# Gated linear attention and a silu feed-forward layer: the fast path's instruction order made with another machine model

## The chip, the cores and the metric

The kernel runs on one core of a Trainium2 chip. The metric is device time in microseconds (us) of one execution, taken as the median of several; a profile is taken of one more execution. The engines are named PE (TensorE, matmuls; PEld are its weight loads), DVE (VectorE), ACT (ScalarE), POOL (GpSimd) and SP (SyncE, which here issues nearly all loads).

## The reference

A gated linear recurrence runs over 768 time steps for 4 batches and 8 heads of width 48; its output, laid out as 3072 tokens of width 384, goes through a feed-forward layer with silu of width 2048.

```python
for t in range(S):
    state = alpha[:, :, t, :, None] * state + np.einsum('bhd,bhe->bhde', k[:, :, t], v[:, :, t])
    y[:, :, t] = np.einsum('bhd,bhde->bhe', q[:, :, t], state)
...
h = x @ w_in
g = h * (1.0 / (1.0 + np.exp(-h)))
return (g @ w_out).astype(np.float32)
```

Everything reaches the chip in wide form: the weights are 64-bit floats that the kernel rounds to 32 bits itself.

## The kernel before

There are two paths. `quotients` is the fast one, valid when the decay factors keep within bounds; it computes a flag `within` while it runs. `general` follows in a conditional that is entered only when the flag says so, which these inputs do not cause. All that the profile shows is `quotients`.

The work is cut into 24 chunks of 128 time steps of one batch (six chunks a batch, the batches taken in turn), and four chunks make a token group; there are six groups. A step of the program's loop handles one chunk in stages:

- `products` transposes alpha, k and q so that time lies along the free axis, scans alpha into running products `u` (L734) and multiplies them into k, which gives `kp` (L745 for early chunks, L749 and L751 later); `quotient` takes reciprocals (L762), scans the inverse, `p` (L764), and multiplies q into it (L770). For the first eight chunks PE transposes (L392). From the ninth on DVE does it (L708, tiles `al` and `turn`), and there is one buffer for `al`, one for `u` and one for `turn`.
- `flip` (from the ninth chunk) writes a transposed `kp` (L780) to DRAM (L782, `flips`), and `land` (L790) reads it back as `kn`.
- `scores` forms the 128 x 128 score blocks on PE; ACT copies them (L812, L818, L821) and POOL masks them (L813, L825). `values` forms the outputs, which ACT copies to `xt` (L863); `states` adds to the recurrent state (L880, DVE).

Between the stages, `fill` issues pieces of the feed-forward layer in proportion to the work that is due. Groups 0 and 1 use plain products with w_in (`enter_plain`, silu L923). Groups 2 to 5 use a scheme with 20 block products in place of 24 (`enter`): it needs sums of blocks of w_in (`sums_w`, tiles `wx` and `w_in`) and of x (`sums_x`, tile `xc`, lines L582 to L587, all on DVE), and combines the products with ACT copies (L950) and DVE additions (L958) before the silu (L955). `PRODUCTS` gives the block of w_in and the block of x of each product. The fourth product, the first of the second piece of `enter`, reads block 15 of x; on PE it follows the first piece and one product of `leave`. Block 15 is the sixth sum of the second part of `sums_x`:

```python
SUMS_X = (
    (9, 1, 2, 1, 4), (6, 1, 0, 1, 2), (7, 1, 2, 1, 3), (8, 1, 0, 1, 7), (10, -1, 1, -1, 8),
    (11, 1, 5, -1, 10), (12, 1, 4, 1, 11), (15, -1, 0, 1, 12), (16, 1, 1, -1, 15),
    ...
PRODUCTS = (
    (11, 9), (3, 6), (14, 6), (18, 15), (5, 11), (17, 8), (9, 14), (7, 10), (10, 3), (19, 12),
```

`leave` multiplies with w_out in seven products per half group, in two PSUM banks (`ps_o`, 192 columns); ACT copies two of them (L1073, L1078), DVE forms u2 (L1088, L1090), u3 (L1099) and the outputs (L1056), and subtracts blocks of g (L1047, L1033 before it). A product that adds into a bank, or starts a new sum in it, waits until the reader of that bank is done.

`audit` reads alpha and the weights once more and reduces their extremes on DVE (L697).

What sets the order: the language's scheduler makes one list per engine, from program order as priority and a simulated run in which a machine model says when an instruction could start. Some instructions are kept in program order by hand: once the early buffers are released (`settle`, after the eighth chunk), all PE instructions are, so PE's order from there is the written one. Sums, audits and a few more are kept likewise; the rest of DVE's, ACT's, POOL's and SP's order is the scheduler's. PE's calls are all recorded at L388 (matmul) and L392 (transpose).

## Time and profile before

| | |
|---|---|
| median of 3 executions | 556.64 us (555.98 to 558.58) |
| the profiled execution | 557.26 us, of which its span is 555.5 us |
| granted PE clock, mean | 0.999 |
| PE busy | 541.4 us (97%), 5026 matmul records |
| weight loads busy | 489.7 us (88%) |
| DVE busy | 445.4 us (80%), 801 instructions |
| ACT, POOL busy | 208.5 us (38%), 76.1 us (14%) |
| DMA | 70.09 MB, mean 126 GB/s |

The span runs from the first instruction to the last; the execution's own time is 1.8 us longer. A group or a row of the timeline gives the start, the busy time, engine, line, operation, the tile written and those read, shapes and the count; in brackets stands the engine's idle time before it and what ended it. One fp32 matmul instruction leaves two records.

### The profile page before, as it was taken

What the parts mean: (1) busy time and instruction counts of PE and PEld (TensorE: products, weight loads), DVE (VectorE), ACT (ScalarE), POOL (GpSimd) and SP (SyncE); (2) the same over time, 40 slices, a digit from 0 to 9 for tenths busy, and PEclk for the clock granted to TensorE, in tenths of its full rate; (3) what the DMA queues carried; (4) which work ended last, traced back from release to release, by engine and by line L of the source; (5) the groups of instructions that cost most, each with busy time, mean ns of one, the idle gap of its engine ahead of it and who ended that gap; (6) DMA issues with size and microseconds to landing.
All of it is one profiled execution on the core that took longest, in us unless ns stands there. A gap on an engine that the chain in (4) does not pass through costs nothing. (4 is left out here: it accounts for less than half of the span.)

```text
span 555.5 us, 12640 instructions
## 1 busy us (share of the span) xinstructions
PE 541.4 (97%) x5026; PEld 489.7 (88%) x5026; DVE 445.4 (80%) x801; ACT 208.5 (38%) x466; POOL 76.1 (14%) x146
## 2 busy tenths in 40 slices
PE   6999999999999999999999999999999999999996
PEld 4788887998899999899999999988998999999996
DVE  5897788974999899997998986998884796945431
ACT  2556653223333253353353353344263342332100
POOL 3210000222210212021011021021121000001000
PEclk9999999999999999999999999999999999999999
DMA  9998971164454625355545654617642135500000
GB/s 215 246 249 210 232 195 33 47 161 116 117 136 125 159 63 138 86 145 149 139 112 139 193 139 120 191 27 183 170 137 91 54 91 169 172 11 22 10 24 30
DMA packets 99217, 70.09 MB, mean 126 GB/s; under 512 B 56272, under 2 KB 88656, under 8 KB 99152
## 3 DMA queue, kind: packets, MB, share of 16 engines
q1 hardware_dynamic: 97232, 65.30, 45.1%
q0 software_dynamic: 1920, 3.93, 2.0%
q8 instruction: 40, 0.66, 0.5%
q14 instruction: 25, 0.20, 0.1%
HBM read 61.34 MB, written 7.86 MB: 125 GB/s over the span
## 5 line engine op out<-in xcount | busy, mean ns | idle before, releaser
L388 PE MATMUL ps_o<-w_out,g 128*128 128x192 f32 x768 | 134.0, 328 | 0.5 <-DVE o L1056 0.5
L388 PEld LDWEIGHTS ps_o<-w_out,g 128*128 128x128 f32 x768 | 125.6, 190 | 3.5 <-DVE o L1056 1.0
L388 PE MATMUL ps_m<-xt,w_in 128*128 128x256 f32 x480 | 113.6, 383 | 1.5 <-ACT xt L863 1.1
L388 PEld LDWEIGHTS ps_m<-xt,w_in 128*128 128x128 f32 x480 | 89.1, 190 | 14.4 <-ACT xt L863 1.6
L388 PE MATMUL ps_o<-wt,g 128*128 128x192 f32 x576 | 99.7, 326 | 0.0
L388 PEld LDWEIGHTS ps_o<-wt,g 128*128 128x128 f32 x576 | 95.1, 190 | 1.6 <-issue 0.2
L388 PE MATMUL ps_m<-xc,w_in 128*128 128x256 f32 x288 | 70.7, 382 | 0.0
L388 PEld LDWEIGHTS ps_m<-xc,w_in 128*128 128x128 f32 x288 | 53.7, 190 | 7.0 <-DVE g L958 0.3
L1047 DVE TENSOR_TENSOR g<-g 128x512 f32<-128x512 f32 x72 | 50.1, 709 | 8.3 <-PE ps_o L388 8.3
L955 ACT ACTIVATE g<-g 128x1024 f32<-128x1024 f32 x32 | 33.1, 1056 | 61.2 <-DVE g L958 61.1
L1059 POOL DMA_DIRECT2D out_dram<-o x40 | 22.0, 551 | 219.5 <-DVE o L1056 113.7
L825 POOL TENSOR_SCALAR_AFFINE_SELECT g<-g 64x256 f32<-64x256 f32 x64 | 34.9, 546 | 124.4 <-ACT g L818 105.7
L388 PE MATMUL ps_m<-xc,wx 128*128 128x256 f32 x192 | 50.1, 383 | 1.0 <-DVE xc L586 1.0
L950 ACT COPY g<-ps_m 128x512 f32<-128x512 f32 x64 | 36.6, 588 | 37.0 <-PE ps_m L388 36.9
L388 PEld LDWEIGHTS ps_m<-xc,wx 128*128 128x128 f32 x192 | 35.2, 190 | 5.2 <-ACT u L1078 1.2
L958 DVE TENSOR_TENSOR g<-ps_m,g 128x512 f32<-128x512 f32 x56 | 37.1, 683 | 3.2 <-PE ps_m L388 2.7
L734 DVE TENSOR_TENSOR_SCAN u<-al,one 128x516 f32<-128x516 f32 x24 | 29.8, 1240 | 11.9 <-ACT al L731 11.6
L923 ACT ACTIVATE g<-ps_m 128x512 f32<-128x512 f32 x32 | 19.1, 597 | 41.7 <-PE ps_m L388 41.4
L950 ACT COPY part<-ps_m 128x512 f32<-128x512 f32 x32 | 18.9, 590 | 38.0 <-PE ps_m L388 24.0
L697 DVE TENSOR_REDUCE seen<-bits 128x1 f32<-128x512 int32 (+1 forms) x33 | 26.3, 823 | 5.7 <-DMA bits<-in_moe_w_in_dram 5.7
L764 DVE TENSOR_TENSOR_SCAN p<-al,inv 128x516 f32<-128x516 f32 x24 | 29.9, 1247 | 1.0 <-PE ps_a L388 0.3
L1056 DVE TENSOR_TENSOR o<-ps_o,u 128x192 f32<-128x192 f32 x24 | 8.5, 355 | 25.7 <-PE ps_o L388 22.8
(129 smaller groups left out, 648.5 us busy)
## 6 DMA issues: line engine op xcount, KB each, us to landing
bits<-in_moe_w_in_dram SPq DMA_DIRECT2D x24, 512.0 KB, 4.7
bits<-in_moe_w_out_dram SPq DMA_DIRECT2D x16, 384.0 KB, 3.9
at<-in_alpha_dram SPq DMA_DIRECT2D x64, 96.0 KB, 2.5
kt<-in_k_dram SPq DMA_DIRECT2D x64, 96.0 KB, 2.6
qt<-in_q_dram SPq DMA_DIRECT2D x64, 96.0 KB, 2.7
bits<-in_alpha_dram SPq DMA_DIRECT2D x9, 512.0 KB, 4.0
out_dram<-o POOLq DMA_DIRECT2D x40, 96.0 KB, 2.4
flips<-turn SPq DMA_DIRECT2D x12, 256.0 KB, 2.4
```

The lines of the kernel that those rows point to most:

```text
L388: in_order(nc.tensor.matmul(*args, **kw))
L697: dve.tensor_reduce(seen[kind][which][:, i : i + 1], x, axis=AX, op=op, apply_absolute_value=True))
L734: dve.tensor_tensor_scan(u[:, end - 1 :: -1], sg[:, end:0:-1], one[:, end:0:-1], 0.0, ALU.mult, ALU.add)
L764: dve.tensor_tensor_scan(p[:, 0:end], sg[:, 0:end], iv[:, 0:end], 0.0, ALU.mult, ALU.add)
L825: gps.affine_select(x, x, pattern=[[0, NP], [1, CH]], compare_op=ALU.is_ge, fill=0.0, base=0, channel_multiplier=-1)
L923: act.activation(gts[grp, h, pair][:, i : i + 2, q % 2, :], ps, AF.Silu)
L950: act.copy(to, ps)
L955: act.activation(x, x, AF.Silu)
L958: dve.tensor_tensor(to, a, b, op)
L1047: dve.tensor_tensor(cells(grp, h, pair, *to), cells(grp, h, pair, *x), cells(grp, h, pair, *y), ALU.subtract)
L1056: dve.tensor_tensor(o, x, y, ALU.add)
L1059: (gps if grp < NG - 1 else nc.sync).dma_start(out[r : r + C, c * HO : (c + 1) * HO], o)
```

## The change

The call of `quotients` moves into a named block of the scheduler, with the option that this block's order is made with the language's other machine model, that of its time-line simulator.

```diff
     args = (q, k, v, alpha, moe_w_in, moe_w_out, out)
-    within = quotients(tc, small, *args)
+    with tc.block(name="quick", schedule_with_timeline_sim=True):
+        within = quotients(tc, small, *args)
     with tc.If(within < 1, label="general"):
         general(tc, *args)
```

The instructions, tiles and buffers are the same. What differs in the built program is the order on each engine, the semaphore values that go with it, and one unconditional branch per engine where the block ends.

## The prediction

> **What bounds the kernel now.** I read the busy line and the slices of the page first.

> ```profile
> PE 541.4 (97%) x5026; PEld 489.7 (88%) x5026; DVE 445.4 (80%) x801; ACT 208.5 (38%) x466; POOL 76.1 (14%) x146
> ...
> PE   6999999999999999999999999999999999999996
> PEld 4788887998899999899999999988998999999996
> DVE  5897788974999899997998986998884796945431
> ```

> TensorE (PE) works from its first transpose at 4.2 us to 550.5 us and is idle almost only in the first and last slice. VectorE (DVE), 80% on the whole, has slices of 9 from about 140 to 420 us. So I asked for busy time by windows there, two rows of which carry the point (us of each engine in 40 us: PE, weight loads, DVE, ACT, POOL):

> ```profile
> 260.00:300.00 40.00, 40.00 (x422) 36.63 (x421) 38.98 (x67) 15.81 (x35) 4.72 (x9) 1.00 0.56 153
> 340.00:380.00 40.00, 39.04 (x376) 35.69 (x378) 35.30 (x65) 17.10 (x40) 6.69 (x12) 1.00 0.45 121
> ```

> Over the seven such windows from 140 to 420 us DVE is busy 258.0 of 280 us: 22 us of slack against PE's 1.8. PE sets the time, and DVE has to deliver in the right order. The view of who waited for whom says how rarely it fails to; PE's longest waits after the start are these:

> ```profile
> PE ps_a L392 <- DMA an<-in_alpha_dram: 4.2, 1, 4.2
> PE ps_m L388 <- ACT xt L863: 1.1, 4, 0.3
> PE ps_m L388 <- DVE xc L586: 1.0, 1, 1.0
> ```

> **What the change moves.** It adds and removes no arithmetic. In the built programs PE's order differs only before about 106 us; from there PE, ACT and POOL have the same order in both, and only DVE and SyncE (SP, which issues the loads) differ. The new DVE order runs the attention preparation ahead as one train: transposed alpha (L708 al) and the scan u (L734) of the next step come early, and the scan p (L764), kp (L749, L751), the transpose of q (L708) and the product p (L770) stand close together, ahead of work that PE asks for sooner. DVE's total stays below PE's, so a move costs only where a result comes after PE wants it. I walked the new order at the places where PE's need is tight, with durations from the trace; DVE instructions start about 0.08 us before the one ahead ends (L1056 at 119.66 takes 0.36, the next starts at 119.94), and I subtract that.

> **Place A, the first output group, 116 to 124 us.** Here are DVE's and PE's rows in the timeline.

> ```profile
> 117.26 0.18 DVE L762 RECIPROCAL inv<-least 128x4 f32<-128x4 f32 x1
> 117.47 1.23 DVE L764 TENSOR_TENSOR_SCAN p<-al,inv 128x516 f32<-128x516 f32 x1
> 118.74 0.36 DVE L1088 TENSOR_TENSOR u<-ps_o,u 128x192 f32<-128x192 f32 x1
> ...
> 116.54 5.47 PE L388 MATMUL ps_o<-w_out,g 128*128 128x192 f32 x32
> 121.85 2.76 PE L388 MATMUL ps_o<-wt,g 128*128 128x192 f32 x16
> ```

> The 32 records are two products of 16 x 163 ns = 2.61 us. The second, at 119.15, adds into the bank that L1088 reads, so it may start when L1088 ends: 119.10, just in time. The new order from L762 is L708 kt, L764, L749, L751, L1088: 1.09 + 1.23 + 0.43 + 0.42 + 0.36 - 0.3 = 3.2 us, so L1088 would end at 120.7. All of it starts 0.9 us later as well: in SP's new order four alpha loads (0.43 us of issue each) stand behind the loads of v, not two. So L1088 ends at about 121.5: PE waits 2.4 us. The next product but one needs the bank that L1056 reads; between L1088 and its end the new order has L708 qt, L1090, L770, L780, L708 al, L1056: 1.10 + 0.36 + 0.68 + 0.71 + 1.14 + 0.36 - 0.5 = 3.9 us, against 2.61 us of product. Another 1.3 us. With some of PE's arrival already later, I take **3.5 us** for A (2 to 4.5).

> **Place B, the sums of x for the fourth token group, 274 to 283 us.** PE's product at 283.38 reads block 15 of x, the sixth sum of its batch (L586).

> ```profile
> 273.87 0.69 DVE L1033 TENSOR_TENSOR g<-g 128x512 f32<-128x512 f32 x1
> ...
> 281.80 0.42 DVE L586 TENSOR_TENSOR xc<-xc,xt 128x256 f32<-128x256 f32 x1
> ...
> 283.38 1.03 PE L388 MATMUL ps_m<-xc,wx 128*128 128x256 f32 x4
> ```

> Before, the sum ends 1.16 us early. The new order puts L708 al behind both L1033, so it no longer fills the wait for ACT's two silus (L955, until 275.03), and the second L1033 starts at 275.1. Behind it stand L764 1.22, L582 0.42, two L880 0.70, L708 al 1.11, L582 0.40, L1047 0.68, L587 0.62, L1047 0.69, L697 1.21, L584 0.62, L749 0.40, L751 0.41, L582 0.41, L708 qt 1.11, L734 1.23, L586 0.42: 11.65 less 16 overlaps of 0.08, plus 0.61 for L1033. It ends at 275.1 + 0.6 + 10.4 = 286.1: PE waits **2.7 us** (1.5 to 4).

> **Place C, the same for the fifth group, 357 to 368 us.**

> ```profile
> 368.38 1.10 PE L388 MATMUL ps_m<-xc,wx 128*128 128x256 f32 x4 [0.96 <-DVE xc L586]
> ```

> This sum is late already: PE was ready at 367.42. The new order has 23 instructions from the second L1033 to L586; among them L764, four audit reductions L697 of 0.63, L708 al, L749, L751, L708 qt, L734 and L770. They sum to 14.5 - 1.8 = 12.7 us, and the second L1033 starts one silu (1.0 us) after the first. In the trace the first starts at 359.73, held back by L708 al; in the new order it waits for the silu alone, which can come between 357.7 (PE's last bank in time for L958) and 359.4 (as now). So L586 ends between 371.4 and 373.1, 4.0 to 5.7 us late, 3.0 to 4.7 more than now. I take **3.6**, nearer to the low end, since the audits no longer stand before L958.

> The third group has 5.6 us of margin (its sum ends at 193.0, PE needs it at 198.6), gets no audit and has one L1033; the sixth has no attention left beside it. I cost both at nothing; a late one would cost what B does.

> **What else moves.** L708 kt reuses the buffer that L780 fills and the store `flips` reads, 2.4 us from issue to landing by the page's DMA lines. Before, some 12 us of DVE work lie between L780 and L708 kt (273.36 to 286.60); in the new order about 2 us (L762, L958, two L1047). DVE will wait there some 0.5 us, twelve times: 6 us, which I cost at nothing since DVE's 22 us of slack covers them; without that cover they are 6 us. SP's loads of kn (L790) go behind those of v, 1.7 us of issue, for a use most of a step (21 us) away: nothing. On the other side the new order computes kp and p earlier, which takes away PE's waits of 0.48 us at 143.83 (for p) and 0.40 in 220:260: -0.9. The reorder before 106 us: PE idles some 2 us there between 10 and 100 us, so it can give or cost 2; I take 0, since every operand's producer order is nearly the same. The block's end adds a branch on each engine; the last store, 2.4 us from 551.2, hides it. Uncovered, it could cost what the nearest row shows, 1.9 us before the last L1056 (PEq L1282).

> Sum: 3.5 + 2.7 + 3.6 - 0.9 = +8.9 us. The profiled execution took 557.26 us (span 555.5), which gives 566.2; the median of the runs, 556.64, lies 0.6 lower: **565.5 us**. With A, B and C at their low ends and the gains at full it is 559.5; at their high ends 571.

> [...] PE's row first: matmuls of 192 columns start every 163 ns, those of 256 every 216 ns, for hundreds of us, so there is no room in a busy PE. [...]

> The second: after PE's last matmul ends (550.5) the granted clock of 553.00:555.50 is 0.76, where it was 1.00; and four transposes take 1.09 to 1.12 us until 14 us, 0.66 from 19.17. So the clock falls after some us of idleness. [...] My sum leaves that out.

> **The rivals.** (1) *The clock falls at C.* For it: the clock rows above; against it: the end needed 2.5 to 5 us of idleness (550.5 to somewhere in 553.0 to 555.5), and C's wait lies between. Price by rows: between nothing and half of the 14 us that the start ran slowly, 7; nearest to 3: 568.5. (2) *The waits for `flips` are not covered* and push every later sum: +6, 571.5. (3) *Nothing lands late*: DVE runs ahead by as much as its new train costs, since it loses no time elsewhere; places A to C vanish, and 556.6 stays. Against it: at B and C the train itself lies between the silu and L586. (4) *Faster*: the earlier kp and p remove PE's waits. Price: the waits of 0.48, 0.40 and 0.96 us after 106 us, and the 2 us before it: -3.9, so 552.7. It decides if A to C together cost under 1 us. (5) A change that does nothing is excluded: the orders differ.

> **How the numbers follow.** Forecast 0.57, clock 0.18, flips 0.08, nothing late 0.12 (no change), faster 0.05. A difference of 0.5% (2.8 us) is about what a measurement of this kernel can tell from none. So faster 0.05, same 0.12, slower 0.83. The range goes from 558, which takes in part of the uncovered middle, to 573, rivals 1 and 2.

> **What would show it.** Right: new PE waits in the changed profile `ps_o <- DVE u L1088` and `o L1056` near 120, `ps_m <- DVE xc L586` of some 3 us near 290 and over 4 near 375; PE's busy time unchanged at 541. Wrong: PE's idle time between 106 and 500 us within 1 us of now. If granted clock under 1.00 shows behind C, rival 1; if L708 waits for DMA flips for more than 10 us in all and PE's waits spread over many steps, rival 2.

## The result, and the profile after

The changed kernel takes 580.21 us (median of four, 578.11 to 582.19) against 556.77 us for the kernel before (555.98 to 558.58): 1.0416 times as long, 95% interval 1.0368 to 1.0463. It is slower by 23.4 us; 8.9 were forecast. The profiled execution took 578.11 us with a span of 576.4 us, 20.9 more than before.

The busy line, the slices of PE and VectorE and the row of the granted clock, from the page of the changed kernel:

```profile
PE 549.3 (95%) x5026; PEld 494.3 (86%) x5026; DVE 445.4 (77%) x801; ACT 208.7 (36%) x466; POOL 75.3 (13%) x146
...
PE   6999999989999999999979899979999999999996
DVE  5986899886989799978996798995983696954431
PEclk9999999989999999999979999999999999999999
```

VectorE's work is the same 445.4 us. PE has dents near 120, 290, 320 and 380 us, and its busy time has grown by 7.9 us with the same 5026 records. Most of that, 6.4 us, lies where the clock was lower: the clock row has an 8 and a 7 at two of the dents. The windows that were quoted for before (us of PE, weight loads, VectorE, ACT, POOL, then the granted clock):

```profile
260.00:300.00 40.00, 35.93 (x306) 31.55 (x305) 35.78 (x63) 15.19 (x36) 5.76 (x11) 0.91 0.54 147
340.00:380.00 40.00, 39.91 (x420) 36.21 (x419) 36.12 (x64) 15.82 (x38) 5.51 (x11) 1.00 0.52 143
```

PE loses 4.1 us of the first window, and in it VectorE is *less* busy than before (38.98). Who waited for whom, PE's rows from 100 us on:

```profile
PE ps_m L388 <- DVE xc L586: 7.4, 2, 3.7
PE ps_m L388 <- DVE g L958: 2.8, 5, 1.6
PE ps_o L388 <- DVE u L1088: 2.6, 1, 2.6
```

L586 and L1088 are the waits that were forecast; L958 was not. The places in the timeline, A, B, one that I call M, and C:

```profile
121.01 1.17 DVE L764 TENSOR_TENSOR_SCAN p<-al,inv 128x516 f32<-128x516 f32 x1
...
122.87 0.36 DVE L1088 TENSOR_TENSOR u<-ps_o,u 128x192 f32<-128x192 f32 x1
...
123.28 4.12 PE L388 MATMUL ps_o<-w_out,g 128*128 128x192 f32 x16 [2.58 <-DVE u L1088]
...
282.33 0.69 DVE L1033 TENSOR_TENSOR g<-g 128x512 f32<-128x512 f32 x1 [0.25 <-ACT g L955]
...
292.87 0.40 DVE L586 TENSOR_TENSOR xc<-xc,xt 128x256 f32<-128x256 f32 x1
293.41 2.04 PE L388 MATMUL ps_m<-xc,wx 128*128 128x256 f32 x4 [3.67 <-DVE xc L586]
...
318.52 0.71 DVE L780 STREAM_TRANSPOSE turn<-kp 128x512 f32<-128x512 f32 x1
...
324.73 1.09 DVE L708 STREAM_TRANSPOSE turn<-kt 128x512 f32<-128x512 f32 x1 [3.20 <-DMA flips<-turn]
327.06 1.13 PE L388 MATMUL ps_m<-xc,w_in 128*128 128x256 f32 x4 [1.56 <-DVE g L958]
...
386.57 1.10 PE L388 MATMUL ps_m<-xc,wx 128*128 128x256 f32 x4 [3.74 <-DVE xc L586]
```

At A and B the train of attention work stands ahead of the result as forecast. At M VectorE itself stands still for 3.20 us: L708 kt wants the buffer that L780 filled, and the store of `flips` has not landed. At A the product that follows takes 4.12 us where one of these takes 2.76: the granted clock was 0.50 from 124.73 to 128.14 us.

Both profiles have 5026 matmul records, so the start of the same record can be subtracted (up to about 106 us, where PE's order differs, that of the record with the same number). This lag of the changed kernel grows in steps; places are given in the changed kernel's time:

| where | growth of the lag, us | of it PE's waiting beyond before | forecast |
|---|---|---|---|
| to 116 us | 1.39 (from -1.00 at 38 us) | | 0 (within 2) |
| A, 117 to 130 us | 4.42 | 2.58 | 3.5 |
| a wait of before gone, about 149 us | -0.55 | -0.48 | -0.9 with another |
| about 275 us | 0.94 | | 0 |
| B, 288 to 305 us | 6.57 | 3.67 | 2.7 |
| M, 320 to 330 us | 2.30 | 1.56 | 0 |
| about 365 us | 0.36 | | 0 |
| C, 380 to 393 us | 4.46 | 2.78 | 3.6 |
| behind 393 us | -0.05 | | 0 |
| behind the last matmul | 1.01 | | 0 |

The sum is 20.85. At A, B and C the lag grows by 1.84, 2.90 and 1.68 us more than PE waited, 6.4 us in all (some 0.16 us at A and at B belongs to the wait itself: the start behind it moves by 2.74 and 3.83 us). The windows view says why. Its windows are cut here where the clock changes; the second number of a row is PE's busy time, the third from the end the granted clock:

```profile
121.32:124.73 3.41, 1.45 (x9) 1.45 (x10) 3.38 (x7) 0.00 (x0) 0.00 (x0) 1.00 0.78 204
124.73:128.14 3.41, 3.41 (x12) 3.33 (x11) 3.34 (x6) 0.00 (x0) 0.56 (x1) 0.50 0.69 206
...
288.57:291.98 3.41, 1.17 (x8) 0.87 (x6) 3.41 (x7) 0.40 (x2) 0.00 (x0) 1.00 0.47 129
291.98:295.39 3.41, 1.98 (x5) 1.65 (x6) 3.41 (x7) 0.00 (x0) 0.00 (x0) 0.50 0.57 179
295.39:298.81 3.42, 3.42 (x10) 2.70 (x9) 3.14 (x8) 1.07 (x2) 0.00 (x0) 0.50 0.54 158
```

Behind a window of 3.41 us in which PE was busy for 1.45 or 1.17 us comes one at half clock, and at B, where PE still waits in that one, a second.

### The profile page after: what moved, and what is told of

Same layout as the page of the kernel before. It is cut to its first block, busy times and chain, and to the rows that moved or that the text cites. A ratio compares the mean times of both kernels' runs of the same rounds, so it can differ in the third digit from the quotient of the medians.

```text
span 576.4 us, 12634 instructions
## 1 busy us (share of the span) xinstructions
PE 549.3 (95%) x5026; PEld 494.3 (86%) x5026; DVE 445.4 (77%) x801; ACT 208.7 (36%) x466; POOL 75.3 (13%) x146
## 5 line engine op out<-in xcount | busy, mean ns | idle before, releaser
L388 PE MATMUL ps_o<-w_out,g 128*128 128x192 f32 x768 | 135.9, 331 | 3.1 <-DVE u L1088 2.6
L388 PEld LDWEIGHTS ps_o<-w_out,g 128*128 128x128 f32 x768 | 127.1, 192 | 6.5 <-DVE u L1088 2.9
L388 PE MATMUL ps_m<-xt,w_in 128*128 128x256 f32 x480 | 114.0, 383 | 2.0 <-ACT xt L863 1.2
L388 PEld LDWEIGHTS ps_m<-xt,w_in 128*128 128x128 f32 x480 | 88.9, 190 | 16.1 <-DVE w_in L647 1.5
L388 PE MATMUL ps_o<-wt,g 128*128 128x192 f32 x576 | 100.5, 327 | 0.0
L388 PEld LDWEIGHTS ps_o<-wt,g 128*128 128x128 f32 x576 | 95.7, 191 | 1.7 <-issue 0.2
L388 PE MATMUL ps_m<-xc,w_in 128*128 128x256 f32 x288 | 72.5, 389 | 1.8 <-DVE g L958 1.8
L388 PEld LDWEIGHTS ps_m<-xc,w_in 128*128 128x128 f32 x288 | 54.6, 193 | 9.4 <-DVE g L958 2.3
L388 PE MATMUL ps_m<-xc,wx 128*128 128x256 f32 x192 | 52.9, 400 | 7.4 <-DVE xc L586 7.4
L1047 DVE TENSOR_TENSOR g<-g 128x512 f32<-128x512 f32 x72 | 49.3, 697 | 9.5 <-PE ps_o L388 9.4
L955 ACT ACTIVATE g<-g 128x1024 f32<-128x1024 f32 x32 | 32.9, 1054 | 49.5 <-DVE g L958 49.5
L825 POOL TENSOR_SCALAR_AFFINE_SELECT g<-g 64x256 f32<-64x256 f32 x64 | 33.5, 524 | 125.0 <-ACT g L818 105.9
L388 PEld LDWEIGHTS ps_m<-xc,wx 128*128 128x128 f32 x192 | 36.7, 199 | 12.7 <-issue 8.3
L958 DVE TENSOR_TENSOR g<-ps_m,g 128x512 f32<-128x512 f32 x56 | 37.9, 685 | 4.1 <-PE ps_m L388 3.5
L734 DVE TENSOR_TENSOR_SCAN u<-al,one 128x516 f32<-128x516 f32 x24 | 29.4, 1224 | 11.0 <-ACT al L731 10.9
L764 DVE TENSOR_TENSOR_SCAN p<-al,inv 128x516 f32<-128x516 f32 x24 | 29.5, 1228 | 6.1 <-PE ps_a L388 5.9
L388 PEld LDWEIGHTS ps_a<-p,kp 48*64 48x64 f32 (+1 forms) x640 | 22.5, 147 | 8.2 <-issue 5.9
L708 DVE STREAM_TRANSPOSE turn<-kt 128x512 f32<-128x512 f32 x16 | 17.8, 1111 | 14.7 <-DMA flips<-turn 9.4
```

Source lines behind the costliest of these rows:

```text
L388: in_order(nc.tensor.matmul(*args, **kw))
L708: dve.transpose(to.rearrange("p g (b j) -> p g j b", j=4), x[:, :, :, 0:32])
L734: dve.tensor_tensor_scan(u[:, end - 1 :: -1], sg[:, end:0:-1], one[:, end:0:-1], 0.0, ALU.mult, ALU.add)
L764: dve.tensor_tensor_scan(p[:, 0:end], sg[:, 0:end], iv[:, 0:end], 0.0, ALU.mult, ALU.add)
L825: gps.affine_select(x, x, pattern=[[0, NP], [1, CH]], compare_op=ALU.is_ge, fill=0.0, base=0, channel_multiplier=-1)
L955: act.activation(x, x, AF.Silu)
```

## The experiments

VectorE's list is changed by hand in most of them. A helper at the end of `quotients` ties the engine's instructions, numbered as the program issues them, into a given order; it adds no wait. The edits below are shortened: `put_ahead`, `put_behind` and `sorted` say how a list was made, while the kernel holds the finished list.

```python
def stand(tc, engine, order):
    ins = [i for i in tc.nc.cur_bb.bb.instructions if i.engine == engine]
    for a, b in zip(order, order[1:]):
        tc.add_manual_dep(ins[b], ins[a].name, edge, reason="order")
```

The kernel before took 556.7 to 557.6 us beside each group of runs; the ratios are to that.

### The block, VectorE's old list, its new list, and a repair

```diff
-    with tc.block(name="quick", schedule_with_timeline_sim=True):
+    with tc.block(name="quick"):
```

> The block without the option: the order of all five engines is that of before, and one branch per engine at the block's end is all that is new. Order theory (the time comes from four results that VectorE delivers late in its new order, at 123, 293, 326 and 386 us of the changed profile, and from the halved clock behind three of these waits): no change, 556.6 us within 1. Block theory (a part of the time is the block itself; behind PE's last matmul the changed profile has 6.1 us to the end of the span, the one before 5.0): 557.7 us, the 1.1 us all behind the last matmul.

557.05 us, ratio 1.0007 (0.9994 to 1.0021). The block costs nothing. The 1.01 us behind the last matmul are not its price: from the last matmul to the end this run has 4.75 us, as the kernel before has, and over all runs it is 4.6 to 5.8 us with a block and without.

```diff
     while done < len(pieces):
         go_on()
+    stand(tc, E.DVE, OLD_ORDER)      # changed kernel, VectorE's list of before
```

> The changed kernel with VectorE's whole order put back to that of before; PE, ACT, POOL and SP keep the order that the other machine model makes beside it. Order theory: the four waits and the halved clock are gone; what can stay is the 1.4 us that PE has lost by 110 us and the 1.1 us at the end: 557 to 559.5 us, mean clock 0.999. Rival (SP's new order of loads delays what VectorE needs, and VectorE only passes it on): most of the 23 us stays, 570 us or more.

561.26 us, ratio 1.0075 (1.0052 to 1.0098). Of the 23.4 us, 19 are VectorE's list. The other 4.4 are more than expected. By the same subtraction of starts against the kernel before, this run has lost 2.49 us at 116 us and 3.54 at 128, and 3.8 for the rest of the way: it is the early part, where the new model has reordered PE, ACT and SP too, and A, where L1088 still comes 0.9 us late.

```diff
+    stand(tc, E.DVE, NEW_ORDER)      # kernel before, VectorE's list of the changed one
```

> The kernel before, without a block, with VectorE's whole order replaced by that of the changed kernel; the default model orders the other engines beside it. Order theory: PE waits again at the four places, clock halved behind three of them, 576 to 579 us, mean clock 0.987 to 0.992. Rival (SP's order of loads): about 557 us. Block theory: 20 us at most of the 23 come back.

596.98 us, ratio 1.0711 (1.0677 to 1.0745): slower than the changed kernel itself. With the loads in the default model's order the new list meets data that are not there. VectorE's waits in this run, the rows that are larger than in the changed kernel (9.4 and 2.7 us there):

```profile
DVE turn L708 <- DMA flips<-turn: 20.7, 5, 5.9
...
DVE al L708 <- DMA at<-in_alpha_dram: 8.4, 2, 6.9
```

So a list of VectorE has its price only together with the order of SP's loads. None of the expectations allowed for that: the order theory said at most 579.

The repair keeps the changed kernel's list and puts the late results ahead of the 3 to 12 instructions that the old list has behind them.

```diff
+    for t in (A_L1088, A_L1090, A_L1056, M_L958, M_L958_2, B_L586, C_L586):
+        put_ahead(NEW_ORDER, t, of=behind(OLD_ORDER, t))
+    stand(tc, E.DVE, NEW_ORDER)
```

> The changed kernel with its own VectorE order, in which six instructions are put ahead of those that the kernel before has behind them: L1088, L1090 and the first L1056 of the first output group, two L958 near 326 us, and L586 for block 15 of x in the fourth and the fifth token group. They step ahead of at most 12 instructions each; all else on VectorE stays in the new order. Order theory: PE's loss at these places, 4.4 + 2.3 + 6.6 + 4.5 = 17.8 us by the start times of the same matmuls in the two profiles, goes: 578.1 - 17.8 = 560.3 us for a profiled execution, 561 to 563 for the median, mean clock 0.998 or more. Rival (VectorE is late everywhere in the new order, by the waits for flips, and these four places only show it): other results come late in their place, 570 us or more.

586.37 us, ratio 1.0536 (1.0503 to 1.0569): a miss, and the wrong way. L586 for block 15 and L1088 did come earlier, but PE now waited 2.9, 5.95 and 5.2 us for other results near 297, 330 and 397 us, and L708 kt for its buffer up to 3.9 us.

### The buffer `turn`

```diff
-        t = late["turn"].tile([128, NP, C], F32, name="turn")...
+        t = late["back"].tile([128, NP, C], F32, name="back")...
```

> The changed kernel, order of all engines as it is, with one difference: L780 (flip) writes into a buffer of its own, so that L708 kt no longer waits until the store of flips has landed in DRAM. Room for it is made by two buffers instead of three for the outputs o and by one tile for u2 and u3. Buffer theory (VectorE stands at L708 kt behind that store, 14.7 us in all in the changed profile, and everything behind it comes late): the waits at L708 for the turn buffer go, PE's wait for L958 at 326 us goes (2.3 us with what follows it), L586 in the fourth group comes at least 1.0 us earlier, and since VectorE gets 14.7 us back the fifth group's wait shrinks too: 560 to 570 us. Order theory (the waits at 123, 293 and 386 us come from the order of the instructions alone): only the 2.3 and the 1.0 us go, 575 us or a little more.

575.61 us, ratio 1.0333 (1.0296 to 1.0370): 0.8% of the time, 4.6 us, better than the changed kernel. L708 kt waits for no store any more, 14.7 us of waiting before, and PE's wait at M is gone. PE's waits in this run (its L1089 is the L1088 of the others):

```profile
PE ps_m L388 <- DVE xc L586: 6.4, 2, 3.7
PE ps_o L388 <- DVE u L1089: 2.5, 1, 2.5
```

The 6.4 us are 2.65 at B and 3.72 at C. So 1.0 us of B's wait came from the store; A and C did not. The order theory's 575 was met.

In the next two only L708 kt is moved, in the new list behind what the old one has ahead of it, and in the old list ahead of what the new one has behind it.

```diff
+    put_behind(NEW_ORDER, each_kt, of=ahead(OLD_ORDER, each_kt))     # changed kernel
...
+    put_ahead(OLD_ORDER, each_kt, of=behind(NEW_ORDER, each_kt))     # kernel before
```

> The changed kernel with VectorE's own new order, in which only each L708 kt is moved: behind all that the kernel before has ahead of it. It then stands 12 to 36 instructions behind L780, which fills the same buffer, where it stood 2 to 9 behind (before: 9 to 32). Buffer theory: VectorE's waits at L708 kt fall from 14.7 us to under 3, and the time to 560 to 566 us. Order theory without the buffer: kt's train of kp, q and p moves with it, so the waits at 123 and 293 us go as well, and nothing tells the theories apart but the waits at L708 and the wait at 326 us. Rival (the attention results now come late for PE's scores): new waits of PE for p or kp (ps_a), over 575 us.

584.29 us, ratio 1.0494 (1.0464 to 1.0524). L708 kt waits for no store at all, and still it is slower than the changed kernel: PE waits 8.9 us for L586 at 393 us. There L708 kt, L764, L708 al, a pair of audit reductions, L749, L751, L708 qt, L734, L770 and a second pair, which itself waits 1.2 us for its data, now all stand between L584 and L586. Neither theory had that; the rival, which looked for late attention results, had the time but not the place.

> The kernel before with its own VectorE order, in which only each L708 kt is moved ahead of all that the changed kernel has behind it: it stands 5 or 6 instructions behind L780. Alpha's transposes and scans stay where they were. Buffer theory: VectorE waits at each kt for the store, 1 to 3 us each, 15 us or more in all, and PE waits behind it at several places, 565 to 585 us. Order theory (the early train of alpha, u and p is what delays L586 and L1088): within 3 us of before, 557 to 560.

614.47 us, ratio 1.1020 (1.0971 to 1.1068), the slowest of all. The row of its waits:

```profile
DVE turn L708 <- DMA flips<-turn: 28.6, 9, 5.3
```

PE waits 26.0 us for L958 in seven places. Five instructions behind L780 is too near: the store takes 2.0 to 5.3 us from issue to landing in the changed profile, and VectorE stands in the meantime with all that PE wants behind it.

### What a wait of PE costs by itself

```diff
+            for _ in range({3: 7, 4: 3, 5: 17}.get(grp, 0) if to == 15 else 0):
+                combine(block_x(grp, to), sa, block_x(grp, a), sb, block_x(grp, b))
```

> The kernel before, its VectorE order kept, with the sum for block 15 of x (L586) repeated on the same operands: 7 times more in the fourth token group, 3 times in the fifth, 17 times in the sixth. Each repeat is 0.34 us, so PE waits about 1.2, 2.0 and 3.1 us for it (the margins before are 1.2, -1.0 and 2.6 us). It measures what a wait of PE costs by itself. If a wait of 2.5 us or more is followed by 3.4 to 6.8 us at half the granted clock, as behind the waits of 2.6, 3.7 and 3.7 us of the changed profile: 1.2 + 1.0 + 3.1 us of waiting and 1.7 to 3.4 us for the third alone, 563.9 to 565.6 us. If the clock follows something else in the new order: 562.2 us and clock 1.0 throughout. If any wait above 1 us suffices: 567 us or more.

572.03 us, ratio 1.0254 (1.0237 to 1.0272). The doses came out larger than meant, 3.05, 2.56 and 5.69 us: a repeat takes 0.45 us, and a scan (L764, 1.22 us) was ordered in between. The clock halved behind all three, for 3.41, 3.41 and 6.83 us. The span grew by 16.1 us, PE's waits by 10.3 (3.05 + 2.56 - 0.96 + 5.69); the other 5.8 go with four intervals at half clock, each of which takes up to 1.7 us of PE's work (half of 3.41). In the old order too, then, the waits were paid in clock as well, 5.8 us on 10.3. The time lies in the range of the last expectation, any wait above 1 us, but all three waits came out at over 2.5 us, so it does not speak for that one. The changed kernel does against it: M's wait of 1.56 us was followed by full clock.

In each run the clock's records lie on one grid of 3.41 us; in the changed kernel half clock stands from 124.73 to 128.14, 291.98 to 298.81 and 387.56 to 390.97 us. PE's idle share of an interval up to the last matmul, by the starts and ends of its records, against the clock of the next:

| PE idle in an interval at full clock | the next interval |
|---|---|
| 0.63 to 1.00 (31 intervals in 11 runs) | half clock, every time |
| 0.58 (three) | half clock twice, full once |
| 0.25 to 0.56 (some 60) | full clock but for two, at 0.34 and, 12 us from the start, at 0.44 |

Half clock followed the intervals at 121.32 (0.58), 288.57 (0.66) and 384.15 us (0.71) of the changed kernel and the one at 372.63 us (0.70) of this run. A wait that the grid cut in two cost no clock in the run `new tail` below, at B again, 3.68 us:

```profile
288.01:291.42 3.41, 1.64 (x11) 1.34 (x9) 3.41 (x7) 0.87 (x3) 0.00 (x0) 1.00 0.49 128
291.42:294.83 3.41, 1.50 (x7) 1.38 (x8) 3.41 (x6) 0.00 (x0) 0.00 (x0) 1.00 0.64 208
294.83:298.25 3.42, 3.42 (x21) 3.27 (x20) 3.42 (x9) 1.56 (x3) 0.00 (x0) 1.00 0.49 156
```

PE was idle for 52% and 56% of two intervals, and the clock stayed at 1.00. In the changed kernel a wait of 2.58 us at A halved it and this one of 3.68 did not.

### Both, and two attempts at a better kernel

```diff
+    both edits: the buffer `back` for the flip, and the repaired list
```

> Both causes taken away: the changed kernel with the flip's buffer of its own (as in the run with two turn buffers) and with the six instructions at the first output group, at 326 us and in the fourth and fifth token group put ahead as in the repair. Theory now (the loss is the order at three places, 2.5, 2.65 and 3.7 us of PE waiting, plus VectorE's waits for the store of flips, plus a clock that halves behind a wait that fills over some 57% of one interval of a 3.41-us grid): PE's waits for L586 fall below 1 us, L1088 to 1.1 at most, none at L958 over 1 us, clock 0.998 or more, 558 to 563 us. Rival (the new order is late wherever VectorE is full, and putting six results ahead makes others late, as it did without the second buffer, 586 us): 570 us or more.

578.40 us, ratio 1.0386 (1.0359 to 1.0414): a miss again, now without any wait for the store. The timeline at C shows what the repair does:

```profile
391.04 0.42 DVE L586 TENSOR_TENSOR xc<-xc 128x256 f32<-128x256 f32 x1
391.61 1.62 PE L388 MATMUL ps_m<-xc,w_in 128*128 128x256 f32 x3 [5.18 <-DVE xc L586]
```

This is the *last* L586 of the batch, for block 14. The sum for block 15 came in time, the train stepped behind it, and so ahead of the next three sums, which PE wants 3 us later. Both repairs moved the loss, and said nothing on its cause.

```diff
+    put_behind(OLD_ORDER, (L734, L737, L708_kt, L749), of=(C_L586,))     # kernel before
+    put_behind(OLD_ORDER, (L1033_at_139,), of=(L770_at_143,))
```

> The kernel before, no block, with VectorE's own order and two local moves: the scan u (L734), L737, L708 kt and L749 of the step at 364 us step behind L586 for block 15 of x in the fifth group, and one L1033 at 139 us steps behind the product p (L770). PE's waits of 0.96 us at 368 and of 0.48 us at 143.8 go: 555.2 us, ratio 0.9974. Rival (the four instructions that step back, 3.1 us, make kp and p of that chunk late, or the sums behind): no change or 1 to 3 us more.

556.84 us, ratio 1.0000 (0.9989 to 1.0011). The waits at 143.8 and 368 us are gone, and the four instructions that stepped back come out as one new wait:

```profile
392.00 1.13 PE L388 MATMUL ps_m<-xt,wx 128*128 128x256 f32 x4 [1.03 <-DVE g L958]
```

```diff
-        t = late["turn"].tile([128, NP, C], F32, name="turn").rearrange(...)      # kernel before
+        c["kn"] = work.tile([128, NP, C], F32, name="kn")
+        t = c["kn"].rearrange(...)
```

> The kernel before, default model, no block, with the flip written into the buffer kn (which the same data come back to from DRAM) in place of turn: no memory is added, and the model may place L708 kt earlier. VectorE has no wait for flips before, so nothing is won by the wait itself: 556.6 us within 2. Rival (the model uses the freedom and moves kt's train ahead of sums that PE wants, as the other model does): slower, 560 us or more, with PE waits for L586 or L958.

558.16 us, ratio 1.0024 (1.0014 to 1.0035): 1.3 us slower, inside the first expectation. No version was found that beats the kernel before.

### Whole stretches of the old list

```diff
+    for i, j in ((169, 187), (406, 497), (521, 592)):
+        NEW_ORDER[i:j] = sorted(NEW_ORDER[i:j], key=OLD_ORDER.index)
```

> The changed kernel; in three stretches of VectorE's list (116 to 128, 268 to 334 and 350 to 396 us of the changed profile) its instructions are sorted by the order of the kernel before. 11, 90 and 66 places change; some 620 of 802 instructions keep the new order, and the buffer turn stays single. Order theory (the loss lies at these places, and the two repairs before only pushed the train of p, al, kp, q, u ahead of the next sums that PE wanted): PE's waits for L1088, L586 and L958 there go, 4.4 + 6.6 + 2.3 + 4.5 = 17.8 us less: 560 to 563 us, clock 0.998. Buffer theory: VectorE's waits at L708 kt in 140 to 268 us, 8 us in the changed profile, stay, and still cost PE little, since they lie where VectorE has slack. Rival (the new order is late wherever one puts a seam): 570 us or more.

> The same three stretches sorted, and the flip's buffer of its own. If the waits for the store cost PE nothing once the stretches are in the old order: the same as the run without the buffer, 560 to 563 us. If they do: faster than that run by what they cost, up to 3.3 us.

574.51 us (ratio 1.0317, 1.0279 to 1.0355) and 574.46 us (1.0321, 1.0289 to 1.0354). Inside the stretches all went as the order theory has it: against the kernel before, the second run's lag is 4.70 us from 236 to 325 us without a step, and 11.4 from 348 to 395. The loss has moved behind the ends of the stretches (a seam below: the place where one order gives way to the other), 6.8 us at 339 and 5.0 at 407 us; so the time that the order theory named was missed. At 339 us in the second run:

```profile
330.32 1.10 DVE L708 STREAM_TRANSPOSE al<-at 128x512 f32<-128x512 f32 x1 [3.30 <-DMA at<-in_alpha_dram]
...
340.20 2.36 PE L388 MATMUL ps_m<-xc,w_in 128*128 128x256 f32 x5 [4.83 <-ACT part L950]
```

The stretch has left to its end what the old list does late, and the new list behind it begins the next steps early. So between the two rows stand two L697, L749, L751, L708 qt, L734, L770 and L780 in one heap, ahead of the L958 that reads `part`. At 407 us the heap is two L708 al, two kt, a qt, two L734, L764, L770 and two pairs of L697. The second buffer makes no difference here (L708 kt waits 11 us in the first of the two runs): those waits fall where VectorE has slack.

```diff
+    NEW_ORDER[521:592] = sorted(NEW_ORDER[521:592], key=OLD_ORDER.index)     # and the buffer `back`
```

> The changed kernel with the flip's buffer of its own and only the last stretch, 350 to 396 us, sorted by the order of before. Order theory: PE's wait of 3.7 us for L586 in the fifth group falls to 1.0 as before, and the rest of that run stays (2.5 us at the first output group, 2.65 in the fourth group): 2.7 us less than with two buffers alone, and up to 1.7 us more where the clock had halved behind this wait: 571 to 573 us. Rival (lateness is carried in from the stretches ahead): no change, 575.6 us.

575.05 us, ratio 1.0331 (1.0286 to 1.0376), against 575.61 with two buffers alone. By the time the rival won. The trace has PE's wait at C down to 0.76 us, as the order theory has it, and a new one of 4.9 us at 409, again right behind the seam.

Two runs without a seam behind the place settle it.

```diff
+    NEW_ORDER[399:] = sorted(NEW_ORDER[399:], key=OLD_ORDER.index)     # from 262 us on
...
+    OLD_ORDER[398:] = sorted(OLD_ORDER[398:], key=NEW_ORDER.index)     # from 257 us on
```

> The changed kernel with its own VectorE order up to 262 us, and from there to the end the remaining VectorE instructions in the order of the kernel before: one seam at 262 us, none behind it. The flip's buffer is not changed. Order theory (the losses of 4.8 and 4.2 us right behind the two ends of the sorted stretches come from the seams, where the attention steps that the new order has run ahead meet in one heap): no loss of PE from 262 us on but the 0.96 us at 368 that the kernel before has too; what is left is the early part and the first output group, some 6 us: 562 to 565 us, clock 0.997 or more behind 130 us. Rival (the lateness is carried in from before 262 us and comes out wherever VectorE is full): 570 us or more.

> The reverse: VectorE's order of before up to 256.7 us, then the remaining instructions in the new order. Order theory: the early part's 3.8 us as in the run with VectorE's whole old order, no loss at the first output group, and behind the seam waits of PE at the fourth and fifth token group of the size of the changed kernel (3 to 4 us each, some 14 us in all with the clock and the wait at 326 us): 573 to 577 us. Rival (lateness is carried in from before): 561 to 565 us.

564.81 us (ratio 1.0134, 1.0114 to 1.0155) and 576.35 us (1.0351, 1.0325 to 1.0377), each inside its range. The old list from 262 us on takes 15.4 us off the changed kernel; the new list from 257 us on adds 15.1 to the run with VectorE's whole old list. In the first the lag stays within 0.1 us of 7.3 from 262 us to the last matmul; in the second PE's waits of 3.68 and 3.72 us for L586 are back at B and C. What lies before 262 us carries nothing into it. And the first shows A as it is without a fall of the clock:

```profile
125.95 2.87 PE L388 MATMUL ps_o<-w_out,g 128*128 128x192 f32 x16 [2.12 <-DVE u L1088]
129.63 2.87 PE L388 MATMUL ps_o<-wt,g 128*128 128x192 f32 x16 [0.82 <-DVE o L1056]
```

## Why the prediction was right and wrong

**Right: places and cause.** The loss was put into VectorE's order, at A, B and C, with L1088, L1056 and L586 as the late results. The old list in place of the new takes 19 of 23.4 us away, and the two runs cut at 260 us put 15 of them behind that point.

**Right: the walk through the order.** A was to cost 2.4 and 1.3 us, 3.5 with a discount. With the clock at full it costs 2.12 + 0.82, and 3.36 by the lag. In the changed kernel the second wait does not show, because the product ahead of it ran at half clock. B was to cost 2.7 us; without the wait for the store it is 2.65. C was to cost 3.0 to 4.7 us more than before, 3.6 taken; it is 2.78 more, a little under the low end. The three sum to 9.8 forecast and 8.8 measured (3.36 + 2.65 + 2.78). It was worth doing by hand, from one trace and the two lists.

**Wrong: "My sum leaves that out".** The clock's fall was named, seen as the first rival, priced at 3 us for C alone and given 0.18. It costs 6.4 us in the profiled execution, at A, B and C; no run shows the 3 us, C alone cost 1.68. The step that failed is "the end needed 2.5 to 5 us of idleness (...), and C's wait lies between": in the trace of before the last matmul ends at 550.8 us, not 550.5, and half clock begins at 554.3, on the grid, so these 3.5 us say little of the shortest wait that halves it. In the table above it went by the idle share of one 3.41-us interval, with 0.58 on either side: some 2.0 us in one interval, as an estimate (0.58 of 3.41). A's 2.58 us was enough. B alone cost 2.90 us, for two intervals.

**Wrong: "which I cost at nothing since DVE's 22 us of slack covers them".** L708 kt waits 14.7 us for its buffer, not 6, and not in twelve equal shares: five waits for `flips`, 9.4 us with one of 3.2, by the releaser's name, the rest under other names; with a second buffer all are gone. The second rival had the mechanism and asked for more than 10 us in all and waits of PE spread over many steps; the first came true if the waits under other names count, the second did not. Slack that is a sum over 280 us does not cover a wait at 272 or 321 us, where VectorE is full and the next L958 or L586 is late already: 1.0 us of B and the 2.30 of M are these waits. Elsewhere they did cost nothing, as forecast. By the medians the second buffer is worth 4.6 us; how much of that is the clock was not told apart. It did not halve in that run's profile, but the mean clock over its four runs, 0.991, is hardly above the changed kernel's 0.990.

**Wrong: "I take 0" for the early part.** With VectorE's list put back, 4.4 us stay (2.9 to 5.5 by the interval), mostly lost before 128 us, more than the bound of 2 that was set. The first 38 us alone differ by up to 3.9 us between two profiles with the same lists of PE and VectorE, so the 1.39 us of the changed profile is no better than that. The clock at the start goes with that difference: its first record at full is at 15.5 us in the changed profile and at 25.4 in that of the repair, where the lag at 38 us is 2.89 in place of -1.00.

**The sum.** Measured in the profile: order 8.8, the store 3.3, the clock 6.4, the early part 1.4, the end 1.0, smaller steps 0.7 (-0.55 + 0.94 + 0.36 - 0.05), less 0.8 for what A's second wait gave up to the clock: 20.8. The median lies another 2.1 us above the profiled execution, which was the quickest of four. Two sums of the prediction are slightly off, and nothing hangs on them: the rival *Faster* adds up to 3.8, not 3.9, and with A, B and C at their low ends, -0.9 and -2 for the early part it is 560.2, not 559.5.

What stays open: why the changed kernel's other three runs are 1.2 to 4.1 us slower than the profiled one. More falls of the clock at A to C are not the reason: their mean clocks, 0.992, 0.987 and 0.992, are none below the profiled run's 0.987. The start could be, since these means leave it out (the run `old tail` has 0.999 with full clock only from 26.3 us on). In the eleven profiles whose PE and SP have the new model's order, full clock first comes 9 to 26 us from the start; the seven that have it at 23.9 us or later lag by 2.1 to 3.3 us at 38 us, the other four by -2.0 to 0.4. In the seven profiles with the old order it comes at 10 to 19 us, and the lag is -1.2 to 0.1. But only one execution of each kernel has a trace, and why the new order should start later was not looked for.

## What to carry to other kernels

A late result is cheap to find: lay the new list against the trace's durations at the few places where the consumer has no margin. Then reckon that a wait of PE can cost clock as well: here waits of 2.56 and 2.58 us did, one of 2.12 us did not, and A, B and C lost 1.84, 2.90 and 1.68 us by it. And charge a wait for a single buffer at the place where it stands, not against slack summed over hundreds of us. And do not judge an order by moving one instruction: what steps back lands on the next result; restore the list from a point to its end, which leaves no seam behind the place.
